# Reversing falling output tiles in device memory, and turning the last output pair around

## Chip, cores and metric

The kernel runs on one core of a Trainium2 chip. The metric is device time in microseconds (us) of one execution; shorter is better. The median of several executions is compared.

## The reference

Two blocks follow each other, for a batch of 4, 768 tokens, 8 heads of 64 (512 columns), all in float32. The first is attention in which a token sees its own and the neighbouring blocks of 32 tokens, the first and last block, and three sampled blocks. The second mixes with a Fourier transform, normalizes, and adds a two-layer network:

```
scores = scale * q @ k.T ; scores[~mask] = -1e9
attn   = softmax(scores) ; x = concat_heads(attn @ v)          # (4, 768, 512)
mixed  = real(fft(fft(x, axis=1), axis=2))
u      = x + mixed
un     = (u - mean(u)) / sqrt(var(u) + 1e-6)                   # per token
out    = u + maximum(un @ w_ch1, 0) @ w_ch2                    # 512 -> 2048 -> 512
```

## The kernel before

Queries of one batch are kept in six tiles of 128 tokens. Their order of rows (`_ORDER`, L53) is chosen for the Fourier step: tiles 0 to 2 are half 0 (tile buffer xA), tiles 3 to 5 half 1 (xB). Tiles 0, 1 and 5 hold tokens in rising order. Tiles 2, 3 and 4 are "falling": partition 0 holds one token, partitions 1 to 126 hold tokens in two interleaved runs that go down, and partition 127 a last one.

Attention of a batch runs in 24 slots (four pairs of heads, six slots each). Beside it the second block of the batch before runs: its steps stand in the queues `apart` (Fourier, normalization, transposes) and `late` (the products of the two layers, `quad` and `channels`), and a planner (`slot`, `gap`, `until`) places them between the attention's products by estimated durations. So all batches but the last share TensorE with the next batch's attention or, for batch 2, run after all attention is done; the last batch runs alone, with `outputs` in place of `channels`. Each engine executes its instructions in the order in which they are written. SP's queue issues nearly all transfers, also in that order: loads of q, k, v, the transposed activations' way through device memory (`far<-un`, L1020, then `unT<-far`, L1032), attention outputs (`row<-oT`, `x<-row`) and the output stores (L1292). It uses eight semaphores in turn, so a transfer also waits for the one eight before it.

`channels(r, half, m)` adds the second layer's product to tile m of one half and, in the last round, calls `store(half, m)`. For the batches before the last, half 0 is stored in the order 2, 0, 1 and half 1 in the order 0, 1, 2. `store` issues one transfer for every part of the tile's row order: a rising tile takes two of 64 rows (tile 5 takes four: 1, 48, 15 and 64 rows), a falling one three: 1 row, 126 rows, 1 row. The 126 rows are written by one transfer whose pattern in device memory has the two runs outermost ([2 runs, 63 rows going down, 512 columns]).

The token tiles xA and xB have two buffers each. `place` (L672, its copy is L681) writes attention outputs of batch b into the buffer of batch b - 2, so `slot` first works off what is left of that batch's half (`until(lambda: (b - 2, 0) in finished)`), and the copy waits for its stores.

In the last batch `outputs(r, m, after)` (L1335) computes a pair of output tiles, m of xA and m of xB, with seven products instead of eight (sums of blocks are formed by VectorE). `OUT` (L1303) gives the order of the pairs: 0, 1, 2 there. The last pair (`ends`) stores each half of the columns as soon as it is done: first xA's left half, then xB's left half (on ScalarE's queue) and right half, last xA's right half. So the last transfer of the program is a falling one (tile 2). After it comes the branch L1805 that skips a general version of the kernel.

Of the kernel before, what the change touches and what calls it, by code (L numbers as in the profile page):

```python
# [11 lines left out]
FP32 = mybir.dt.float32  # L12
# [5 lines left out]
ALU = mybir.AluOpType  # L18
# [62 lines left out]
def _rows(view, tile):  # L81

    got = []
    for t, p0, runs, jump, n, s0, step in _ORDER:
        if t != tile:
            continue
        at = view[s0:s0 + 1, :]
        row, col = list(at.ap[0])[0], list(at.ap[1])
        if jump > 0 > step:
            got.append((p0, runs * n, bass.AP(tensor=at.tensor, offset=at.offset,  # L90
                                              ap=[[jump * row, runs], [step * row, n], col])))
            continue
# [8 lines left out]
def kernel(  # L101
# [14 lines left out]
    nc = tc.nc  # L116

    B, H, S, D = q.shape
    DM = H * D
    FF = w_ch1.shape[1]  # L120
    P = 128
# [9 lines left out]
    T = C // 2  # L131
# [170 lines left out]
    def bit(n):  # L302
# [5 lines left out]
                      in_=bass.AP(tensor=_words(sampled_blocks, NB * NR), offset=0,  # L308
                                  ap=[[0, NB], [1, 2 * NB * NR]]))
# [138 lines left out]
    for w, w_sb in ((w_ch1, w1_sb), (w_ch2, w2_sb)):  # L448
        rows, cols = w.shape
        words = _words(w, rows * cols)  # L450
        for row in range(rows // P):
            for col in range(0, cols, WN):
                src = bass.AP(tensor=words, offset=2 * (row * P * cols + col),
                              ap=[[2 * cols, P], [1, 2 * WN]])
# [527 lines left out]
    z_at = [0.0, 0.0]  # L982
    rstd_at = deque()
    finished = set()
    folded = set()

    def mixer(b, xA, xB):
# [4 lines left out]
        tt = nc.vector.tensor_tensor  # L992
# [51 lines left out]
        t, s = {}, {}  # L1044
# [243 lines left out]

        def store(half, m, cols=slice(0, DM), queue=nc.sync):
            x = (xA, xB)[half]  # L1290
            for p0, cnt, rows in _rows(out[b][:, cols], T * half + m):
                queue.dma_start(out=rows, in_=x[p0:p0 + cnt, m, cols])  # L1292
            if cols.stop == DM:
                stored[half] += 1
            if stored[half] == T:
                finished.add((b, half))

        stored = [0, 0]
        last = b == B - 1
        OUT = (0, 1, 2) if last else (2, 0, 1)  # L1303
        out_of = (OUT, OUT if last else (0, 1, 2))
        o_t, o_s = {}, {}
        DH = DM // 2

        def block(r, k, n):
            return w2_sb[:, 8 * r + 4 * k:8 * r + 4 * k + 4, n * DH:n * DH + DH]
# [25 lines left out]
        def outputs(r, m, after):  # L1335

            if m == OUT[0]:
                output_left(m, 1)
                output_left(m, 2)
            a11, a12, a21, a22 = (hs[g, i][:, :, m * P:(m + 1) * P]  # L1340
                                  for i in range(2) for g in range(2))
            a0, a1 = xA[:, m, 0:DH], xA[:, m, DH:DM]
            b0, b1 = xB[:, m, 0:DH], xB[:, m, DH:DM]
            rights = {j: [o_t[j, 0], o_t[j, 1]] for j in (1, 2, 3, 4)}

            def product(pool, tag, a, c):
                ps = pool.tile([P, 512], FP32, tag=tag, name="yy")[:, 0:DH]
                for k in range(4):
                    nc.tensor.matmul(ps, a[:, k, :],  # L1349
                                     c[k // 2][:, k % 2, :] if isinstance(c, list) else c[:, k, :],  # L1350
                                     start=(k == 0), stop=(k == 3))
                busy("PE", 1.75)
                return ps

            def plus(to, a, c=None):
                tt(out=to, in0=a, in1=to if c is None else c, op=ALU.add)
                busy("DVE", 0.43)

            def ahead(j):
                if after is not None:  # L1360
                    output_left(after, j)

            ends = r == 1 and after is None
            u = sum_p.tile([P, DH], FP32, tag="oT", name="u")
            p1 = product(ps_m, "m", a11, block(r, 0, 0))
            nc.scalar.copy(out=u, in_=p1)
            plus(a0, p1)
            plus(a0, product(ps_m, "m", a12, block(r, 1, 0)))
            if ends:
                store(0, m, slice(0, DH))  # L1370
            if m == OUT[0]:
                output_left(m, 3)
                output_left(m, 4)
            plus(u, product(ps_t, "t", a21, rights[2]), u)
            plus(a1, u)
            plus(b0, product(ps_s, "s", a22, rights[4]))
            plus(u, product(ps_s, "s", o_s[m, 3], rights[3]), u)
            both = xB[:, m, :].rearrange("p (n d) -> p n d", n=2)
            tt(out=both, in0=both,
               in1=u.rearrange("p (o d) -> p o d", o=1).broadcast_to([P, 2, DH]), op=ALU.add)  # L1380
            busy("DVE", 0.7)


            if ends:
                store(1, m, slice(0, DH), nc.scalar)
            p5 = product(ps_o, "o", o_s[m, 1], rights[1])
            plus(b1, p5)
            if r == 1:
                store(1, m, slice(DH if ends else 0, DM))
            plus(a1, p5)  # L1390
            ahead(1)
            ahead(2)
            ahead(3)
            p3 = product(ps_m, "m", o_s[m, 4], block(r, 1, 1))
            plus(a1, p3)
            if r == 1:
                store(0, m, slice(DH if ends else 0, DM))
            ahead(4)

        fl = [[("tm"[h == 1 and m != 0], lambda h=h, m=m: un_flip(h, m), 0.6, 0.55, 0.0)  # L1400
# [10 lines left out]
              for m, us in (((1, 2), RIGHT), ((0,), COMBINE))]  # L1411
        le = [("d", lambda i=i: left(0, i), 0.0, 0.0, COMBINE) for i in (1, 3, 4)]
        after = ([fl[0][1], sp[1][1]] + le +
                 [fl[0][2], sp[1][2], wh[1][1], fl[0][0], sp[1][0], wh[1][2],
                  fl[1][1], fl[1][2], wh[1][0]] + ri[0] + [fl[1][0]] + ri[1])
        if not last:
# [13 lines left out]
        for r in range(0 if last else NF // 4):  # L1430
# [21 lines left out]
    needed = set()  # L1452
    state = {"paired": False, "total": None, "w": 0, "got": 0, "owed": 0.0, "ready": 0.0,
             "back": 0.0, "place": None,
             "alone": False, "drain": lambda: None}

    def channel_step():
        masks["by_pe"] = False
# [62 lines left out]
    def until(met, alone=False):  # L1521

        state["alone"] = alone
        while not met():
            if late:
                channel_step()
                soon = state.pop("soon", None)
                gap(2.0, start=soon)
            else:
                do_apart()  # L1530
        state["alone"] = False
# [24 lines left out]
    def w_loads():  # L1556
        while state["got"] < min(len(wchunks), state["w"] + len(W_ROOMS)):
            w_load(state["got"])
            state["got"] += 1

    def w_steps(sl):
        while state["w"] < min(len(wchunks), W_PACE * sl):
            w_round(state["w"])
            state["w"] += 1

    def slot(sl):
        phase, r = divmod(sl, SB)
        n, s = divmod(sl, SP)
        units = range(SLOT * sl, SLOT * sl + SLOT)
# [55 lines left out]
        if s >= ((4 if late else 5) if reuse else 3) and (n, 0) in oT_at and once(n):  # L1625
            b, j = pairs[n]
            at = oT_at[n, 0]
# [12 lines left out]
        if sl < B * SB and n % NP == 1 and s == 1:  # L1640
            b = pairs[n - 1][0]
            at = oT_at[n - 1, 1]
            if b >= 2:
                until(lambda: (b - 2, 1) in finished)
                at = when["PE"] + LEAVES
# [46 lines left out]
        while short and (not more or soon) and (  # L1692
# [5 lines left out]
            short.remove(item)  # L1698
            item[2]()
        w_loads()  # L1700
        w_steps(sl)
        table_step(sl)

# [32 lines left out]
    begin(B - 1)  # L1736
    state["drain"] = lambda: None
    until(lambda: len(finished) == 2 * B, True)
    ordered.close()

    def general():
# [4 lines left out]
        for b in range(B):  # L1748
            xs = [xp.tile([P, T, DM], FP32, tag=tag, name="x") for tag in ("xA", "xB")]
            for h in range(H):  # L1750
                qt = ld.tile([P, C, 2, D], FP32, tag="q", name="qg")
                for t in range(C):
                    for p0, cnt, rows in _rows(q[b, h], t):
                        nc.sync.dma_start(out=qt[p0:p0 + cnt, t, 0, :], in_=rows)
                nc.sync.dma_start(out=qt[:, :, 1, :],
                                  in_=k[b, h].rearrange("(p c) d -> p c d", p=P))
                vt = ldv.tile([P, C, D], FP32, tag="v", name="vg")
                nc.sync.dma_start(out=vt, in_=v[b, h].rearrange("(p c) d -> p c d", p=P))
                for half in range(2):
# [4 lines left out]
                    sl = slice(half * HS, (half + 1) * HS)  # L1764
# [3 lines left out]
                op = ps_o.tile([P, C, D], FP32, tag="o", name="og")  # L1768
                rs = sm.tile([P, C, 1], FP32, tag="r", name="rs", bufs=2)
                for t in range(C):  # L1770
                    s = ps_s.tile([P, 2, 512], FP32, tag="s", name="sg")
# [29 lines left out]
                step[1]()  # L1801
            for fn, _ in rest:
                fn()

    with tc.If(over > 0):  # L1805
        general()
# [37 lines left out]
```

## Time and profile before

| what | value |
|---|---|
| median of 3 runs | 1046.56 us (1045.99 to 1046.66) |
| the profiled execution | 1045.29 us, its span 1043.6 us |
| granted TensorE clock, mean | 0.994 |
| TensorE matmuls busy | 1018.6 us (98%) |
| VectorE, ScalarE, GpSimd busy | 683.2, 359.3, 257.7 us |
| transfers | 58.06 MB in 163582 packets, mean 56 GB/s |
| output stores (L1292) | 71 issued by SP, 4 by ScalarE |
| output stores of batch 0, 1, 2, 3 begin at | 389.6, 633.1, 866.3, 1010.0 us |

The span is the time from the first to the last instruction. A line of the timeline has start, length, engine, line of the kernel, operation, output and inputs, and in brackets how long the engine stood idle before it and what released it. SPq is SP's queue.

### The profile page before, as it was taken

Reading aid. Unit: us, or ns where it says so; the run is one execution under the profiler, and the core shown is the slowest. Engines: PE = TensorE matmul, PEld = TensorE weight load, DVE = VectorE, ACT = ScalarE, POOL = GpSimd, SP = SyncE. Lnnn points to the kernel's source line nnn. Section 1 sums busy time; section 2 is a strip of 40 time slices with the busy share of each in tenths; the row PEclk is TensorE's granted clock in tenths of the full one; section 3 lists DMA queues with packets and bytes.
Section 4 is the critical chain, followed back from the end, with each engine's and each line's share of the span. In section 5 each row is a group of like instructions: output and inputs, shape, how many; then the busy total and the mean of one; then the engine's idle time right before and its main releaser. Section 6 shows DMA issues by size and latency. Waiting matters only on the chain.

```text
span 1043.6 us, 12498 instructions
## 1 busy us (share of the span) xinstructions
PE 1018.6 (98%) x4382; PEld 537.0 (51%) x4382; DVE 683.2 (65%) x1246; ACT 359.3 (34%) x727; POOL 257.7 (25%) x287
## 2 busy tenths in 40 slices
PE   8999999999999999999999998999999999999996
PEld 4444345435565454444535653444444764578575
DVE  6899895978745646655677367665458475674663
ACT  6998765563021012433341111253220221210210
POOL 1000173662000203545560003256540221000000
PEclk9999999999999999999999999899999999999998
DMA  7767422291000143322320005521010001000001
GB/s 213 225 190 234 99 47 46 51 153 25 1 1 20 41 58 65 73 47 45 63 46 1 1 20 101 91 48 43 17 23 8 0 1 42 20 0 1 1 19 45
DMA packets 163582, 58.06 MB, mean 56 GB/s; under 512 B 144298, under 2 KB 154296, under 8 KB 163512
## 3 DMA queue, kind: packets, MB, share of 16 engines
q1 hardware_dynamic: 162216, 56.46, 24.1%
q10 hardware_dynamic: 1264, 0.72, 0.3%
q8 instruction: 36, 0.59, 0.2%
q14 instruction: 34, 0.28, 0.1%
q0 software_dynamic: 32, 0.01, 0.0%
HBM read 43.80 MB, written 13.37 MB: 55 GB/s over the span
## 4 chain that ended last, share of the span: by engine, by line
PE 84%; DVE 8%; DMA 2%; ACT 2%; SPq 2%; issue 1%; ACTq 0%; DVEq 0%
PE y L1281 20%; PE z L1116 16%; PE s L583 11%; PE o L657 9%; PE yp L1116 8%; PE yy L1349 7%; PE xp L1116 4%; PE zp L865 2%; PE sp L728 1%; PE s L593 1%; DMA far<-un 1%; ACT e L603 1%; DVE t L1070 1%; PE yz L1224 1%; DVE acc L638 1%
## 5 line engine op out<-in xcount | busy, mean ns | idle before, releaser
L643 POOL TENSOR_TENSOR acc<-acc,e 128x384 f32<-128x384 f32 x160 | 163.4, 1054 | 126.3 <-DVE e L613 106.7
L583 PE MATMUL s<-qT,kT 64*128 64x384 f32 x768 | 154.5, 518 | 9.5 <-DVE e L613 5.4
L657 PE MATMUL o<-e,vr 128*64 128x384 f32 x768 | 141.7, 497 | 0.0
L1281 PE MATMUL y<-w_sb,hB 128*128 128x512 f32 x264 | 118.9, 601 | 0.0
L1281 PE MATMUL y<-w_sb,hA 128*128 128x512 f32 x264 | 117.1, 595 | 0.0
L613 DVE TENSOR_TENSOR e<-s,mask 128x768 f32<-128x768 f32 x86 | 78.3, 950 | 53.9 <-ACT s L611 45.9
L583 PEld LDWEIGHTS s<-qT,kT 64*128 64x128 f32 x768 | 64.4, 187 | 90.0 <-ACT e L603 22.7
L1284 DVE TENSOR_TENSOR x<-y,x 128x512 f32<-128x512 f32 x66 | 45.6, 691 | 98.3 <-PE y L1281 98.1
L611 ACT ACTIVATE s<-s 128x768 f32<-128x768 f32 x86 | 65.1, 791 | 107.3 <-PE s L583 107.2
L603 ACT ACTIVATE e<-s 128x768 f32<-128x768 f32 x106 | 81.0, 814 | 54.2 <-PE s L593 32.9
L643 POOL TENSOR_TENSOR acc<-e 128x384 f32<-128x384 f32 x42 | 48.7, 1180 | 201.5 <-ACT e L603 121.9
L1116 PE MATMUL z<-unT,t 128*128 128x384 f32 x256 | 93.1, 486 | 0.0
L657 PEld LDWEIGHTS o<-e,vr 128*64 128x64 f32 x768 | 47.9, 136 | 69.4 <-issue 67.0
L1281 PEld LDWEIGHTS y<-w_sb,hB 128*128 128x128 f32 x264 | 49.6, 192 | 62.0 <-issue 61.3
L1121 DVE TENSOR_TENSOR hA<-z,hA 128x384 f32<-128x384 f32 x64 | 35.7, 557 | 69.8 <-PE z L1116 69.7
L1281 PEld LDWEIGHTS y<-w_sb,hA 128*128 128x128 f32 x264 | 49.2, 190 | 59.5 <-issue 55.7
L1125 ACT ACTIVATE hA<-hA 128x384 f32<-128x384 f32 x64 | 33.5, 523 | 121.8 <-DVE hA L1121 121.8
L1116 PEld LDWEIGHTS z<-unT,t 128*128 128x128 f32 x256 | 48.6, 190 | 34.1 <-DVE hA L1121 0.4
L1125 ACT ACTIVATE hB<-hB 128x384 f32<-128x384 f32 x64 | 33.5, 523 | 86.0 <-DVE hB L1121 86.0
L1136 ACT COPY hA<-xp 128x384 f32<-128x384 f32 x32 | 15.3, 477 | 129.3 <-PE xp L1116 129.3
L1116 PE MATMUL z<-t,w_sb 128*128 128x384 f32 x128 | 46.7, 487 | 1.5 <-DVE t L1070 1.5
L1116 PE MATMUL xp<-unT,w_sb 128*128 128x384 f32 x128 | 47.2, 492 | 0.0
(236 smaller groups left out, 1440.4 us busy)
## 6 DMA issues: line engine op xcount, KB each, us to landing
wraw<-in_moe_w_ch_dram SPq DMA_DIRECT2D x32, 512.0 KB
vr<-in_v_dram SPq DMA_DIRECT2D x30, 192.0 KB
far<-un SPq DMA_DIRECT2D x18, 256.0 KB
unT<-far SPq DMA_DIRECT2D x24, 192.0 KB
qb<-in_q_dram SPq DMA_DIRECT2D x44, 96.0 KB
kb<-in_k_dram SPq DMA_DIRECT2D x44, 96.0 KB
out_dram<-x SPq DMA_DIRECT2D x11, 252.0 KB
out_dram<-x SPq DMA_DIRECT2D x19, 128.0 KB
```

The lines of the kernel that those rows point to most:

```text
L583: nc.tensor.matmul(s[:, i, 0:HS], kT[rows, c * P:(c + 1) * P], qT[rows, queries], start=True, stop=u not in by_pe)
L603: nc.scalar.activation(out=e, in_=s[:, :, 0:HS], func=ACT.Exp, scale=scale)
L611: nc.scalar.activation(out=s[:, :, 0:HS], in_=s[:, :, 0:HS], func=ACT.Exp, scale=scale)
L613: nc.vector.tensor_tensor(out=e, in0=s[:, :, 0:HS], in1=m.broadcast_to([P, 2, HS]), op=ALU.mult)
L643: nc.gpsimd.tensor_add(out=acc[:, i, :], in0=start[:, i, :], in1=e[:, i, :])
L657: nc.tensor.matmul(o[D * i:D * i + D, :], vt[:, i, c, :], e[:, i, :], start=(c == 0), stop=(c == C - 1))
L1116: nc.tensor.matmul(to, a[:, k, :], c[:, k, :], start=(k == 0), stop=(k == ND // 2 - 1))
L1121: tt(out=to, in0=ps, in1=a, op=ALU.add)
L1125: nc.scalar.activation(out=h, in_=h, func=ACT.Relu)
L1281: nc.tensor.matmul(y, hs[0, half][:, l, m * P:(m + 1) * P], w2_sb[:, 4 * r + l, :], start=(l == 0), stop=(l == 3))
L1284: nc.vector.tensor_tensor(out=x[:, m, :], in0=y, in1=x[:, m, :], op=ALU.add)
L1349: nc.tensor.matmul(ps, a[:, k, :], c[k // 2][:, k % 2, :] if isinstance(c, list) else c[:, k, :], start=(k == 0), stop=(k == 3))
```

## The change

- `store` of a falling tile (2, 3, 4) of batches 0 to 2 no longer writes the output. `turn_round` writes its 128 rows to a scratch tensor in device memory, where the rows stand in the reverse order of the output: the pattern is [2 runs, 64 rows, 512 columns]. The rows of partition 0, which belong to the far end of the run, are written by single-row transfers: to the scratch tensor (tiles 2 and 5), or straight to the output (tile 3).
- When a half's tile 2 (`m == T - 1`) is stored, a copy `fall` is owed. It copies 128 rows (half 0) or 256 rows (half 1) from scratch to the output, device memory to device memory, with a row step of -1 in the output; its patterns have two halves of the columns outermost ([2 halves, n rows, 256 columns]). It goes out on SP's queue ahead of the next `store`, or at the end of a later slot.
- Single-row parts of a store are issued after the larger ones.
- The last batch takes its pairs in the order 2, 0, 1, so that the last pair is tiles 1 (rising, xA) and 4 (falling, xB). In that pair the products come in another order: xB's halves are finished and stored first (both on ScalarE's queue), then xA's right half, then its left half. Falling tiles of the last batch are stored as before.

```
+    owed = deque()
 ...
         def store(half, m, cols=slice(0, DM), queue=nc.sync):
             x = (xA, xB)[half]
-            for p0, cnt, rows in _rows(out[b][:, cols], T * half + m):
+            while owed:
+                owed.popleft()[1]()
+            falls = T * half + m in (T - 1, T, T + 1) and not last
+            if falls:
+                turn_round(half, m)
+            for p0, cnt, rows in sorted(_rows(out[b][:, cols], T * half + m), key=lambda i: -i[1]):
+                if falls and (cnt > 1 or p0 or m):
+                    continue
+                if not last and half == 1 and m == T - 1 and cnt == 1:
+                    rows = falling[1][2 * P:2 * P + 1, :]
                 queue.dma_start(out=rows, in_=x[p0:p0 + cnt, m, cols])
+            if not last and m == T - 1:
+                owed.append((state["slot"], lambda: fall(half)))
 ...
+        def turn_round(half, m):
+            if half not in falling:
+                falling[half] = far_p.tile([(1 + half) * P + 1, DM], FP32, tag=f"fall{half}",
+                                           name="falls", bufs=2)
+            rows = falling[half]
+            x = (xA, xB)[half][:, m, :]
+            at = rows[m * half * P:m * half * P + 1, :]
+            nc.sync.dma_start(out=bass.AP(tensor=at.tensor, offset=at.offset,
+                                          ap=[[DM, 2], [2 * DM, P // 2], [1, DM]]), in_=x)
+            if half == 0:
+                nc.sync.dma_start(out=rows[P:P + 1, :], in_=x[0:1, :])
+
+        def fall(half):
+            n = (1 + half) * P
+            src, to = falling[half][1:2, :], out[b][S // 2 * (1 + half) - 1:S // 2 * (1 + half), :]
+            nc.sync.dma_start(
+                out=bass.AP(tensor=to.tensor, offset=to.offset,
+                            ap=[[DM // 2, 2], [-DM, n], [1, DM // 2]]),
+                in_=bass.AP(tensor=src.tensor, offset=src.offset,
+                            ap=[[DM // 2, 2], [DM, n], [1, DM // 2]]))
 ...
-        OUT = (0, 1, 2) if last else (2, 0, 1)
+        OUT = (2, 0, 1)
 ...
+            if r == 1 and after is None:
+                plus(u, product(ps_t, "t", a21, rights[2]), u)
+                plus(a1, u)
+                plus(u, product(ps_s, "s", o_s[m, 3], rights[3]), u)
+                tt(out=both, in0=both,
+                   in1=u.rearrange("p (o d) -> p o d", o=1).broadcast_to([P, 2, DH]), op=ALU.add)
+                busy("DVE", 0.7)
+                plus(b0, product(ps_s, "s", a22, rights[4]))
+                store(1, m, slice(0, DH), nc.scalar)
+                p5 = product(ps_o, "o", o_s[m, 1], rights[1])
+                plus(b1, p5)
+                store(1, m, slice(DH, DM), nc.scalar)
+                plus(a1, p5)
+                plus(a1, product(ps_m, "m", o_s[m, 4], block(r, 1, 1)))
+                store(0, m, slice(DH, DM))
+                plus(a0, product(ps_m, "m", a12, block(r, 1, 0)))
+                store(0, m, slice(0, DH))
+                return
 ...
     def slot(sl):
+        state["slot"] = sl
 ...
         w_loads()
+        while owed and owed[0][0] < sl:
+            owed.popleft()[1]()
         w_steps(sl)
```

More of the change, by code (lines that the diff above doesn't have):

```diff
@@ L1290, in store @@
             x = (xA, xB)[half]
-            for p0, cnt, rows in _rows(out[b][:, cols], T * half + m):
+            while owed:
[8 more added lines that the diff above has]
+                    rows = falling[1][2 * P:2 * P + 1, :]
                 queue.dma_start(out=rows, in_=x[p0:p0 + cnt, m, cols])
-            if cols.stop == DM:
-                stored[half] += 1
-            if stored[half] == T:
+            if not last and m == T - 1:
+                owed.append((state["slot"], lambda: fall(half)))
+            stored[half] += cols.stop - cols.start
+            if stored[half] == T * DM:
                 finished.add((b, half))
+        falling = {}
+        def turn_round(half, m):
[17 more added lines that the diff above has]
+                            ap=[[DM // 2, 2], [DM, n], [1, DM // 2]]))
         stored = [0, 0]
         last = b == B - 1
-        OUT = (0, 1, 2) if last else (2, 0, 1)
+        OUT = (2, 0, 1)
         out_of = (OUT, OUT if last else (0, 1, 2))
@@ L1361, in ahead @@
                     output_left(after, j)
-            ends = r == 1 and after is None
             u = sum_p.tile([P, DH], FP32, tag="oT", name="u")
+            both = xB[:, m, :].rearrange("p (n d) -> p n d", n=2)
             p1 = product(ps_m, "m", a11, block(r, 0, 0))
@@ L1367, in outputs @@
             plus(a0, p1)
+            if r == 1 and after is None:
[16 more added lines that the diff above has]
+                return
             plus(a0, product(ps_m, "m", a12, block(r, 1, 0)))
-            if ends:
-                store(0, m, slice(0, DH))
             if m == OUT[0]:
@@ L1377, in outputs @@
             plus(u, product(ps_s, "s", o_s[m, 3], rights[3]), u)
-            both = xB[:, m, :].rearrange("p (n d) -> p n d", n=2)
             tt(out=both, in0=both,
@@ L1381, in outputs @@
             busy("DVE", 0.7)
-            if ends:
-                store(1, m, slice(0, DH), nc.scalar)
             p5 = product(ps_o, "o", o_s[m, 1], rights[1])
@@ L1388, in outputs @@
             if r == 1:
-                store(1, m, slice(DH if ends else 0, DM))
+                store(1, m)
             plus(a1, p5)
@@ L1396, in outputs @@
             if r == 1:
-                store(0, m, slice(DH if ends else 0, DM))
+                store(0, m)
             ahead(4)
@@ L1454 @@
              "back": 0.0, "place": None,
-             "alone": False, "drain": lambda: None}
+             "slot": 0, "alone": False, "drain": lambda: None}
     def channel_step():
@@ L1738 @@
     until(lambda: len(finished) == 2 * B, True)
+    assert not owed
     ordered.close()
@@ L1803, in general @@
                 fn()
+            while owed:
+                owed.popleft()[1]()
     with tc.If(over > 0):
```

## The prediction

> **What bounds the kernel now.** I read the page first (busy shares), then the waits, then the timeline around each group of output stores, and last the trace's records of DMA packets and of the semaphore increments with which a transfer lands.
>
> ```profile
> PE 1018.6 (98%) x4382; PEld 537.0 (51%) x4382; DVE 683.2 (65%) x1246; ACT 359.3 (34%) x727; POOL 257.7 (25%) x287
> ```
>
> TensorE is busy 98% of the span and works in a fixed order, so only what makes it idle, or what follows its last product, can move the time. Gaps between matmul records sum to 16.9 us; the longest by far is 4.52 us at 648.80. The view of the copy `place` (L681, PSUM to the token tile x) names what it waits for:
>
> ```profile
>   DMA far<-un: 8.7, 1
>   PE xt L680: 2.6, 4
>   DMA out_dram<-x: 1.9, 1
> ```
>
> The timeline around the long one (start us, length us, engine, line, operation; in brackets the idle time before it), SP's queue and then ACT and TensorE:
>
> ```profile
> 635.09 0.35 SPq L1020 DMA_DIRECT2D far<-un  x1
> 636.49 1.19 SPq L1292 DMA_DIRECT2D out_dram<-x  x2
> 637.79 0.53 SPq L1020 DMA_DIRECT2D far<-un  x1
> 641.98 3.96 SPq L1032 DMA_DIRECT2D unT<-far  x4
> 645.98 1.94 SPq L1292 DMA_DIRECT2D out_dram<-x  x2
> ```
>
> ```profile
> 650.26 0.48 ACT L681 COPY x<-xt 128x384 f32<-128x384 f32 x1 [8.70 <-DMA far<-un]
> 650.64 0.85 ACT L540 ACTIVATE kb<-kb 128x768 f32<-128x768 f32 x1
> ...
> 653.32 2.93 PE L583 MATMUL s<-qT,kT 64*128 64x384 f32 x8 [4.52 <-DVE e L613]
> ```
>
> The copy writes the xA buffer of batch 1, so it needs that batch's half-0 stores done. The last two (645.98 and 647.32) landed at 649.69 and 650.01; the copy follows 0.25 later. The name far<-un is wrong here: that transfer landed at 650.63. Behind the copy, in ACT's order, stand a square and the next exponential, then DVE's masking, then TensorE's scores: copy to scores is 3.06 us. So in this stage (call it batch 1) the end is set by SP's queue. Batch 0 has the same place with a little slack:
>
> ```profile
> 400.00 0.48 ACT L681 COPY x<-xt 128x384 f32<-128x384 f32 x1 [1.90 <-DMA out_dram<-x]
> ...
> 402.55 2.80 PE L657 MATMUL o<-e,vr 128*64 128x384 f32 x16
> ...
> 405.27 1.56 PE L583 MATMUL s<-qT,kT 64*128 64x384 f32 x8
> ```
>
> The stores landed at 399.40 and 399.71. TensorE is not idle; with 3.1 us from copy to scores the copy could start at 402.15 before the scores at 405.27 move. Slack: 2.15 us.
>
> **How stores of falling rows run.** A 126-row falling store shows two late semaphore increments, a 64-row one sixteen, a 15-row one fifteen: the count of DMA engines follows the outermost count in device memory (2, 64, 15), for 126 rows as such would allow 14. Alone, issue to landing is 7.9 us (633.38 to 641.29) against 2.3 to 2.9 for 64 rows. Packets on those two engines: 2 KB each 79 ns, 1 KB each 44 ns when queued up, plus 1.9 us of stalls for a store that starts fresh (1011.50 to 1018.41 is 6.9, 63 x 0.079 is 5.0). The other transfers use all 16 engines, so each has a share waiting behind these two: far<-un of 635.09 landed after 6.83 us, others of its kind after 2.6.
>
> **The change, part by part.**
>
> *Falling tiles to scratch (`turn_round`).* 128 rows again with an outermost count of 2: 64 packets of 2 KB per engine instead of 63, landing after 8.0 us. Per batch SP issues 15 instead of 17; its queue has gaps around these stores, so that is worth nothing.
>
> *The copy back (`fall`).* New: device memory to device memory, outermost count 2 on both sides, 1 KB packets, 128 per engine for half 0 and 256 for half 1. The Trainium skill, page "DMA: Bandwidth & Descriptors", section "Why a DMA increments its semaphore by 16 and not by 1", gives the engine count as the largest number up to 16 that divides the slowest dimension of both access patterns. By that rule these copies sit on two engines as well, which no row here shows for this kind of transfer; it speaks against the change. Price per packet: not below 44 ns (1 KB, SBUF to device memory); not above 88 (reading and writing one after the other). The v loads read 1.5 KB in 61 ns spacings, reading and writing together, so I take 44. The same page, section "Latency and other measured facts", has device-to-device copies at 207 to 214 GB/s each way over 16 engines; from this I estimate 79 ns, and by it the sum below would be about +35 us.
>
> *Its place in SP's queue.* half 0's `fall` is owed after tile 2's store, which comes first (order 2, 0, 1), and `store` issues what is owed before its own transfers. So it stands ahead of tile 0's and tile 1's stores, waits for `turn_round` to land, and its data stand ahead of theirs on engines 0 and 1. Exactly those stores release the copy L681.
>
> Batch 0. `turn_round` lands by 398.5 (before: 398.33, 398.51). `fall` issues at 398.6; first packet 1.3 later (1010.23 to 1011.50), 399.9. 128 x 0.044 + 1.9 of stalls: 407.5. Tile 0 and 1: 16 packets x 0.079: 408.8; landing 0.3: 409.1. Before 399.7, so 9.4 late; less slack 2.15: **7.2 us** of new TensorE idling. After the 4.52 us gap the granted clock is 0.50 from 652.3 to 659.1; the 5.8 us of work in it lose 2.9. A gap of 7 should do the same: **2.9**. Bounds: 5.0 (no stalls, no clock loss) to 15.7.
>
> ```profile
> 640.00:653.00 13.00, 8.80 (x41) 3.51 (x37) 8.10 (x11) 4.24 (x8) 4.42 (x4) 0.97 0.77 150
> 653.00:655.00 2.00, 1.68 (x6) 1.03 (x8) 1.13 (x2) 1.19 (x3) 0.00 (x0) 0.50 1.18 175
> ```
>
> (The column before the last two is the granted clock.)
>
> Batch 1. `turn_round` issued 633.06, landed 641.2; `fall` issues 641.3, packets 642.6 to 650.2. Behind it on the two engines: tile 0's store 0.64, far<-un 0.64, four unT<-far (96 packets of 128 B each per engine, 11.7 ns: 4.5), tile 1's store 0.64, landing 0.3: 656.9. Before 650.0: **6.9 us**, no slack; the clock loss is paid already. Bounds 4.7 to 12.5. What follows (unT<-far of half 1, kb loads) is shifted along with TensorE.
>
> Half 1's `fall` (256 packets, some 13 us) is issued at the end of the next slot. The qb load behind it (680.26) is wanted at 700.30, row<-oT ahead of a normalization after 783: hidden by that slack; if it were gone, up to 9 us. Batch 2 runs its stores with nothing waiting; no cost, except that no slot follows, so its half-1 `fall` is issued by the last batch's first store.
>
> *The end.* Before:
>
> ```profile
> 1034.22 3.32 SPq L1292 DMA_DIRECT2D out_dram<-x  x7
> ```
>
> ```profile
> 1033.57 1.89 PE L1349 MATMUL yy<-w_sb,os 128*128 128x256 f32 x8
> ...
> 1035.50 0.42 DVE L1356 TENSOR_TENSOR x<-yy,x 128x256 f32<-128x256 f32 x1 [0.97 <-PE yy L1349]
> ```
>
> The falling store issued at 1036.34 ends its packets at 1041.27; SP passes that wait at 1041.71, 1.3 us after it could (its branch at 1037.60 takes 2.55 until 1040.15); the span ends 1.9 later. With tile 1 last, two 64-row stores end it: SP branches at 1037.1 and nothing is left to wait for: 1.7 us gained, were engines 0 and 1 free. The seven products keep their durations; one 0.18 us wait for a PSUM bank goes, which the branch covers. But from 1011.2 the engines have: `fall` 256 x 0.044 + 1.9, tile 2 and tile 3 falling 5.0 each, tile 5 and tile 0 0.63 each, tile 4 in two halves on ACT's queue 5.6, the last two stores 0.4: 30.5 us, to 1041.7, where it was 1041.3. So **+0.4**; bounds -1.7 to +11.5.
>
> Sum: 7.2 + 2.9 + 6.9 + 0.4 = 17.4 us. The profiled execution took 1045.29 (span 1043.6 and 1.7 around it), 1.27 under the median of 1046.56; so about 1062.7 for such an execution and 1064.0 as median.
>
> **Rivals.**
> 1. *Everything on sixteen engines* (128 rows divide by 16, 126 don't). It decides if `turn_round` lands before 636.5, some 3 us after issue as 64-row stores do. Then far<-un lands at 637.7, unT<-far starts 3 us earlier, the gap at 648.80 shrinks by 3.0 and no longer halves the clock (2.9), and the end gives 1.7: 7.6 gained, 1039. Against it: the [63,2] stores that used two engines though 126 has divisor 14. Chance 0.08.
> 2. *Copy back on sixteen, `turn_round` on two.* Only SP's wait is left: batch 0 stores land at 403.5 (3.8 late, 1.65 after slack), batch 1 starts unT<-far at 643.7 instead of 641.98 (1.7), the end gives 1.7: +1.7, 1048.2. Nothing speaks for the difference between the two transfers but their kind. Chance 0.06.
> 3. *The copies L681 are not what binds* and the delays hide; only the end counts: 1045 to 1047. Against it: both copies start 0.25 to 0.29 after the stores land. Chance 0.05.
>
> The forecast keeps 0.81.
>
> **How the numbers follow.** About 0.2% (2 us) can be told from no change. Faster: rival 1 and a little of rival 3, 0.09. Same: rival 2 and the rest of 3, 0.10. Slower 0.81. The forecast's own bounds are 5.0 + 4.7 - 1.7 = 8.0 (1054.6) and 15.7 + 12.5 + 11.5 = 39.7 (1086). Reading and writing overlap in the v loads, so I stop at 1080 above; below, 1051 takes in some hiding not seen. Left out: the rivals and the top, 2 in 10.
>
> **What would show it.** Right: L681's DMA waits grow to about 11 and 15.6 us; a gap of some 7 us before the scores at 405 with granted clock 0.50 behind it; the gap at 649 near 11 us; `fall` landing some 9 and 15 us after issue, with two late increments; the last stores landing near 1042 plus the shift. Wrong: `fall` with sixteen increments, or tile 1's stores landing within 2 us of where they did against the products around them.

## The result, and the profile after

The changed kernel takes 1071.34 us (median of 4 runs, 1071.17 to 1071.61) against 1046.34 of the kernel before on the same chip: ratio 1.0239, 95% interval 1.0222 to 1.0257. The forecast was 1064.0 with a range of 1051 to 1080, so direction and range hold, and the middle is 7 us too low.

The page, its line of busy times:

```profile
span 1069.5 us, 12491 instructions
...
PE 1021.1 (95%) x4382; PEld 538.3 (50%) x4382; DVE 683.4 (64%) x1246; ACT 359.6 (34%) x727; POOL 258.0 (24%) x287
```

TensorE does the same 4382 products, in the same order up to the pairs of the last batch, in 2.5 us more busy time; the span is 25.9 us longer. So most of the loss is idle time, and the start of the i-th matmul in one trace can be subtracted from its start in the other. By the times of the trace of before, that difference stays within 0.1 us of 0 up to the product at 405.27, is 5.81 there and 8.74 from 408.6 on, stays there until 653.32, jumps to 14.98, and is 14.5 from 659 to the last product. Behind the last product, 8.1 us to the end of the span became 19.5. Three places, then, to the hundredth: 8.74 + 5.72 + 11.42 = 25.88.

The copy into the token tile (L681) names the first two:

```profile
  DMA far<-un: 14.9, 1
  DMA out_dram<-x: 9.8, 1
  PE xt L680: 2.6, 4
```

Before, these were 8.7 and 1.9. The timeline of batch 0 (start, length, engine, line, operation, output and input; in brackets the idle time before it), SP's queue, then ACT and TensorE:

```profile
389.84 0.74 SPq L1322 DMA_DIRECT2D falls<-x  x1
390.62 0.91 SPq L1325 DMA_DIRECT2D falls<-x  x1
398.30 0.66 SPq L1331 DMA_DIRECT2D out_dram<-falls  x1
399.06 3.76 SPq L1302 DMA_DIRECT2D out_dram<-x  x4
```

```profile
407.97 0.48 ACT L681 COPY x<-xt 128x384 f32<-128x384 f32 x1 [9.79 <-DMA out_dram<-x]
...
411.08 1.65 PE L583 MATMUL s<-qT,kT 64*128 64x384 f32 x4 [5.67 <-DVE e L613]
```

SP issues nothing from 391.5 to 398.30: it waits for `turn_round` (issued 389.84, landed 398.28). `fall` lands at 406.35, and the stores of tiles 0 and 1, issued behind it, at 406.68 to 407.66 instead of 399.71 at the latest. The copy starts 0.31 after the last of them, the scores 3.11 after the copy. Then the half clock (the column before the last two):

```profile
411.00:413.00 2.00, 1.92 (x6) 1.14 (x8) 0.89 (x2) 1.11 (x4) 0.00 (x0) 0.50 0.67 130
413.00:415.00 2.00, 2.00 (x6) 0.54 (x3) 1.00 (x2) 1.37 (x2) 0.00 (x0) 0.50 0.40 63
```

Batch 1, which begins 8.7 later than in the trace of before:

```profile
641.80 0.56 SPq L1322 DMA_DIRECT2D falls<-x  x1
...
649.86 0.66 SPq L1331 DMA_DIRECT2D out_dram<-falls  x1
650.62 2.11 SPq L1302 DMA_DIRECT2D out_dram<-x  x2
652.83 0.53 SPq L1021 DMA_DIRECT2D far<-un  x1
653.47 7.36 SPq L1033 DMA_DIRECT2D unT<-far  x4
660.93 1.82 SPq L1302 DMA_DIRECT2D out_dram<-x  x2
```

```profile
665.24 0.48 ACT L681 COPY x<-xt 128x384 f32<-128x384 f32 x1 [14.93 <-DMA far<-un]
...
668.30 1.01 PE L583 MATMUL s<-qT,kT 64*128 64x384 f32 x2 [10.76 <-DVE e L613]
```

The last two stores of tile 1 land at 664.79 and 665.02 (before: 649.69 and 650.01, so 6.3 late when the 8.74 of batch 0 are taken off), and the copy follows 0.22 behind. The name far<-un in the bracket is again not the releaser: that transfer landed at 665.62, after the copy had begun.

The end, SP's queue and ACT's over the last batch, and then SP's alone as it stands in a window that begins at 1035:

```profile
1024.46 40.34 SPq L1302 DMA_DIRECT2D out_dram<-x  x16
1045.23 3.52 ACTq L1302 DMA_DIRECT2D out_dram<-x  x6
```

```profile
1050.44 14.36 SPq L1302 DMA_DIRECT2D out_dram<-x  x13
```

Sixteen stores from 1024.46, of which thirteen begin at 1050.44 or later: SP issued three and then stood still for 24 us. SP's waits between 1024 and 1066 (total, times, longest) put that down to an earlier store that had to land, not to the data:

```profile
SPq L1302 <- DMA out_dram<-x: 30.5, 4, 24.3
```

At 1050.44 the last product was over (1049.92), and four of the last batch's six tiles had still to be issued; the last transfer landed at 1066.38.

### The profile page after: what moved, and what is told of

It is laid out like the page before. It is cut to its first block, busy times and chain, and to the rows that moved or that the text cites. A ratio compares the mean times of both kernels' runs of the same rounds, so it can differ in the third digit from the quotient of the medians.

```text
span 1069.5 us, 12491 instructions
## 1 busy us (share of the span) xinstructions
PE 1021.1 (95%) x4382; PEld 538.3 (50%) x4382; DVE 683.4 (64%) x1246; ACT 359.6 (34%) x727; POOL 258.0 (24%) x287
## 4 chain that ended last, share of the span: by engine, by line
PE 83%; DVE 7%; ACT 3%; DMA 2%; SPq 2%; issue 1%; ACTq 0%; DVEq 0%
PE y L1282 20%; PE z L1117 15%; PE s L583 11%; PE o L657 9%; PE yp L1117 8%; PE yy L1385 6%; PE xp L1117 4%; PE zp L865 2%; PE sp L728 1%; PE s L593 1%; ACT e L603 1%; DMA far<-un 1%; DVE t L1071 1%; PE yz L1225 1%; DVE acc L638 1%
```

## Experiments

**The theories.** A: the 14.5 us in the middle come from where half 0's copy back stands (in SP's queue, and on its two DMA engines) ahead of the stores that release L681; the 11.4 us at the end have another cause, a semaphore. The trace's records give, for each transfer, the semaphore that it raises and those that it waits for. SP's fourth store of the last batch (the one row of tile 5) waits for semaphore 117 and starts at 1050.44. The transfer before it on 117 is not SP's: it is ScalarE's store of xB's left half, issued at 1045.23, landed at 1050.42. So the eight semaphores are not for SP's queue alone, as the description of the kernel has it: they serve the transfers of both queues in turn, in the order in which the built program lists them. For the last batch the records give the turn as 117 ScalarE (126 rows), 100 SP (64), 102 ScalarE (1), 111 SP (48), 112 ScalarE (1), 113 SP (15), 115 ScalarE (126), 116 ScalarE (1), 117 SP (1). ScalarE's stores of the last pair stand ahead of and between SP's stores of tile 5, which are ready 20 us earlier. Why the built program lists them so early is not shown. Rivals: the added traffic itself costs, wherever it stands (middle); falling rows back up on two engines, or the new last pair costs as such (end).

| run | last matmul ends | end of span behind it | median | ratio to before, 95% interval |
|---|---|---|---|---|
| before | 1035.5 | 8.1 | 1045.3 to 1046.5 | 1 |
| after | 1049.9 | 19.5 | 1071.34 | 1.0239, 1.0222 to 1.0257 |
| end_on_sp | 1049.9 | 6.5 | 1057.88 | 1.0118, 1.0103 to 1.0134 |
| fall_late | 1034.9 | 19.8 | 1057.30 | 1.0114, 1.0098 to 1.0129 |
| scratch_alone | 1050.6 | 12.9 | 1065.45 | 1.0184, 1.0168 to 1.0201 |
| last_pair_alone | 1034.9 | 8.3 | 1044.74 | 0.9991, 0.9982 to 1.0000 |
| round16 | 1042.3 | 8.1 | 1049.48 | 1.0031, 1.0019 to 1.0043 |
| fall16 | 1039.2 | 6.4 | 1047.91 | 1.0017, 1.0008 to 1.0027 |
| both16 | 1032.4 | 8.3 | 1042.35 | 0.9962, 0.9949 to 0.9975 |
| late_both16 | 1030.3 | 8.1 | 1040.12 | 0.9943, 0.9930 to 0.9957 |
| late_on_sp | 1035.6 | 6.3 | 1043.28 | 0.9976, 0.9967 to 0.9985 |
| last_pair_on_sp | 1034.9 | 7.5 | 1044.33 | 0.9992, 0.9983 to 1.0001 |
| late_both16_moved | 1030.1 | 6.4 | 1038.10 | 0.9927, 0.9914 to 0.9941 |

(us; the first two columns of numbers are from each kernel's profiled execution, the ratios are to the kernel before on the same chip. The ranges of "before" are its medians on the chips used here. The profiled executions lie within 0.9 us of their kernel's median, but round16's is its slowest, 1052.19, 2.7 above the median.)

### end_on_sp: the last pair's stores on one queue

```
-                store(1, m, slice(0, DH), nc.scalar)
+                store(1, m, slice(0, DH))
 ...
-                store(1, m, slice(DH, DM), nc.scalar)
+                store(1, m, slice(DH, DM))
```

> As the changed kernel, but the last pair's two xB stores go out on SP's queue instead of ScalarE's. Theory A (the extra 11.5 us behind the last product come from SP standing still: its tile-5 transfer waits for the completion semaphore that was handed to a ScalarE store which is issued only at 1045): with all stores on one queue no transfer waits for a later one, the time from the last matmul to the end of the span falls from 19.6 us to 6 to 9 us, and the median to 1058 to 1061. Rival B (the end is a backlog of falling rows on two DMA engines): the same rows fall, so the 19.6 us stay within 2 us and the median within 1069 to 1072. By both the TensorE gaps at 405 (5.7 us) and 657 (10.8 us) stay.

Measured: the last matmul ends where it did, both gaps stand (5.79 and 11.03 us), and the end shrinks from 19.5 to 6.5 us. The median is 0.1 under the range given. SP's stores of the whole last batch, and its waits for earlier stores between 1024 and 1052:

```profile
1024.48 27.05 SPq L1302 DMA_DIRECT2D out_dram<-x  x22
```

```profile
SPq L1302 <- DMA out_dram<-x: 0.5, 1, 0.5
```

Twenty-two stores in 27 us instead of sixteen in 40; the longest stretch without an issue, 7.9 us up to 1036.62, is a wait for a tile that DVE finishes. The rows, their patterns and their two engines are those of the changed kernel; rival B falls.

### fall_late: the copy back behind the stores

```
-            while owed:
+            while owed and half == 1:
                 owed.popleft()[1]()
```

> As the changed kernel, but half 0's copy back is no longer issued ahead of the stores of tiles 0 and 1: it goes out at the end of the next slot. Theory A (what delays both middle stages is the place of the copy back in SP's queue and on its two engines ahead of the stores that release L681): tile 0's and 1's stores land where they did before, the gap at 405 goes, the one at 649 is again about 4.5 us, the last matmul ends within 2 us of 1035.5, and the median is 1056 to 1059, the end keeping its 19 to 20 us (ScalarE's stores still hold semaphores that SP waits for). Rival B (the cost is the added traffic itself: 2.4 MB more, and two engines busy for 8 us more): the copy runs 10 us later into the next loads, at least half of the 14.5 us stays, median 1064 or more.

Measured: the gap at 405 is gone, the one at 649 is 4.11 us, the last matmul ends at 1034.9; all 14.5 us are back, with the same traffic. SP's queue in batch 0:

```profile
396.54 1.11 SPq L1302 DMA_DIRECT2D out_dram<-x  x2
398.59 0.69 SPq L1331 DMA_DIRECT2D out_dram<-falls  x1
```

The stores at 396.54 land at 399.40 and 399.71, to the hundredth as before the change, and `fall` goes out behind them; it still takes 8.45 us. Rival B falls here too. The end keeps its 19.8 us:

```profile
1009.41 40.63 SPq L1302 DMA_DIRECT2D out_dram<-x  x16
1030.17 3.56 ACTq L1302 DMA_DIRECT2D out_dram<-x  x6
```

This run shows the semaphore's mechanism a second time, at another transfer. The built program's order differs a little, so SP now stands one transfer earlier, before the 15-row store of tile 5; and the same holds in scratch_alone, where ScalarE stores parts of tile 5 as before the change and SP stands before tile 1's first store. From the records of the three traces:

```
kernel         SP's store that stood    semaphore  ScalarE's store before it on that semaphore
after          1 row,   start 1050.44   117        126 rows, issued 1045.23, landed 1050.42
fall_late      15 rows, start 1035.36   117        126 rows, issued 1030.17, landed 1035.34
scratch_alone  64 rows, start 1050.45   112        64 rows,  issued 1048.34, landed 1050.38
```

### scratch_alone and last_pair_alone: each half of the change by itself

scratch_alone has `turn_round` and `fall`, with `OUT`, `ends` and the last pair as in the kernel before:

```
-        OUT = (2, 0, 1)
+        OUT = (0, 1, 2) if last else (2, 0, 1)
```

> The reversal through device memory alone; the last batch's order of pairs and its last pair as before the change. Theory A: both middle gaps as in the changed kernel (last matmul 14 to 15 us later than before), and behind it SP still waits once for a semaphore that a ScalarE store holds (here before tile 1's stores), so that the last falling halves start some 3 us later against the last product: median 1062 to 1066. Rival B (what costs at the end is the new last pair): the end is that of before, 8.1 us behind the last matmul, median 1060 to 1061.

last_pair_alone stores the tiles of batches 0 to 2 as before, and has the new last pair:

```
-            if cols.stop == DM:
-                stored[half] += 1
-            if stored[half] == T:
+            stored[half] += cols.stop - cols.start
+            if stored[half] == T * DM:
 ...
-        OUT = (0, 1, 2) if last else (2, 0, 1)
+        OUT = (2, 0, 1)
```

> The new order of pairs and the new last pair alone; output tiles of batches 0 to 2 stored as before the change. Theory A (the last pair itself gains, since the last transfers are 64-row ones; its loss came with the way in which the copy back changed the semaphores): all matmuls but the last pair's where they were, the end 6 to 8 us behind the last matmul instead of 8.1, median 1044 to 1046.5. Rival B (the new last pair costs, whatever the stores before it): 19 us behind the last matmul, median 1057 to 1058.

Measured: the reversal alone has both gaps (5.89 and 10.89 us) and, without the new last pair, still 12.9 us at the end instead of 8.1. Rival B of that run (the end as before) falls. The new last pair alone costs nothing: median 1.0 us lower, an interval that just touches no change. In the turn of the semaphores, ScalarE's stores (102 to 116) here come behind all of SP's stores of the other tiles, and no transfer waits for a later one. The products end 0.6 us earlier in the profiled execution, but 0.56 of this is there before the last pair begins, so the pair's products save 0.04. Its end is 8.3 us, not the 6 to 8 expected: the falling half stored last from ScalarE's queue (issued 1032.46) lands after 8.50 us, and SP's 64-row stores, issued around it, after 5.2 to 5.9.

### round16, fall16 and both16: which two-engine transfer costs what

All three start from end_on_sp. round16 writes `turn_round` as two transfers whose outermost count is 64:

```
+            for r in range(2):
-            nc.sync.dma_start(out=bass.AP(tensor=at.tensor, offset=at.offset,
-                                          ap=[[DM, 2], [2 * DM, P // 2], [1, DM]]), in_=x)
+                nc.sync.dma_start(out=bass.AP(tensor=at.tensor, offset=at.offset + r * DM,
+                                              ap=[[2 * DM, P // 2], [1, DM]]),
+                                  in_=x[r * P // 2:(r + 1) * P // 2, :])
```

> As end_on_sp (last pair's stores on SP's queue), and turn_round writes its 128 rows as two transfers of 64 rows, which use sixteen DMA engines; the copy back stays on two. Theory A (the sum: SP waits 8 us for turn_round to land, then the copy back holds two engines for 8 us ahead of the stores that release L681): turn_round lands 3 to 3.5 us after its issue, the copy back then takes its 8 us from 393.5 to 401.5 in batch 0, so tile 0's and 1's stores land by 402.5, about the end of the slack: gap at 405 at most 1 us. In batch 1 the stores land within 4 us of before. Median 1043 to 1049. Rival C (it is the copy back alone that costs, wherever it starts): the gaps shrink by no more than 2 us each and the median stays at 1053 or more.

fall16 cuts the columns of `fall` into 16 parts instead of 2, on both sides:

```
-                            ap=[[DM // 2, 2], [-DM, n], [1, DM // 2]]),
+                            ap=[[DM // 16, 16], [-DM, n], [1, DM // 16]]),
```

> As end_on_sp, and the copy back is cut into sixteen column parts (128 bytes a packet), so that sixteen engines do it; turn_round stays on two. Theory A: only SP's wait for turn_round is left; tile 0's and 1's stores of batch 0 land 4 to 6 us later than before, less 2.15 us of slack: 2 to 4 us; batch 1 1.7 to 4 us: median 1047 to 1053. Rival D (the copy back costs by its bytes and packets, 2048 of them for half 0 instead of 256, not by the number of its engines): it lands 8 us or more after its issue, as in end_on_sp, and the median stays within 3 us of 1058 or goes above it.

both16 has both edits.

> As end_on_sp with both: turn_round as two transfers of 64 rows and the copy back in sixteen column parts; its place in SP's queue stays ahead of the stores. Theory A: turn_round lands after 3 to 3.5 us, the copy back 3 to 5 us after that, no TensorE gap at 405; in batch 1 far<-un and unT<-far no longer stand behind falling rows on two engines, so the gap of 4.5 us at 649 shrinks and may vanish: median 1037 to 1043, under the kernel before. Rival D (copies in device memory cost by their packets): 1046 or more.

Measured: in fall16 the copy back lands 3.6 us after its issue, with sixteen increments, for 2048 packets of 128 bytes, and the gap at 405 is 1.74 us; rival D falls. The Trainium skill, page "DMA: Bandwidth & Descriptors", section "Why a DMA increments its semaphore by 16 and not by 1", has the engine count follow the slowest dimension; these runs agree, for copies in device memory too (outermost 2: two late increments, outermost 16: sixteen). In round16 the copy back takes 8.14 us as before, and here the expectation missed: the gap at 405 is 3.20 us and not at most 1, because `turn_round` lands 5.5 us after its issue, not 3 to 3.5. Fifteen of its increments come within 3.9 us (the transposed activations' loads of 388 are still in front of it), the last one 1.6 us later; a packet of 16 KB that loads instructions takes 1.45 us from 392.63 on, but the records don't name its engine, so that it held up this one is an inference. The copy back then starts at 395.62 and the stores land at 405.06. Its median lies 0.5 over the range given; rival C, with 1053 or more, falls all the same. In both16 the two transfers' terms vanish, and the gap of the kernel before shrinks as well:

```profile
651.25 2.35 PE L583 MATMUL s<-qT,kT 64*128 64x384 f32 x8 [2.58 <-DVE e L613]
```

By the end of the last matmul in the profiled executions, from both16 (1032.4): the copy back on two engines costs 9.9 us (round16, its slowest execution), `turn_round` on two 6.8 (fall16), both on two (end_on_sp) 17.5. Medians less the end behind the last matmul give 7.4, 7.5 and 17.4. Each of the two costs some 7 us or more; how nearly they add is open.

### late_on_sp and late_both16: the place

late_on_sp has the edits of fall_late and of end_on_sp; late_both16 has these and both of sixteen engines.

> The two single corrections together: half 0's copy back at the end of the next slot (as fall_late), and the last pair's stores on SP's queue (as end_on_sp); falling rows and the copy back still on two DMA engines. Theory A (two separate causes): the last matmul ends at 1034.9 as in fall_late, the span 6.5 us behind it as in end_on_sp: span 1041.4, median 1042.5 to 1044.5. Rival E (the two share something, two engines that are full at the end): the sum isn't reached, median 1046 or more.

> As both16, with half 0's copy back issued at the end of the next slot instead of ahead of the stores of tiles 0 and 1. Theory A: all three causes are gone; no gap at 405, in batch 1 only what the loads and the exponentials behind them need, the end 6.5 us behind the last product: median 1036 to 1042. Rival D: the 2048 small packets hold all sixteen engines while the next loads want them, and the median is 1044 or more.

Measured: late_on_sp has the end of the last matmul of fall_late (within 0.8 us) and the end of end_on_sp, and comes out 0.24% under the kernel before: the two causes are separate, and they are all of the loss. late_both16 leaves 1.35 us of the gap at 649, and the granted clock stays at 1.00 behind it:

```profile
649.52 1.78 PE L583 MATMUL s<-qT,kT 64*128 64x384 f32 x8 [1.35 <-DVE e L613]
```

```profile
  DMA far<-un: 5.5, 1
  PE xt L680: 2.5, 4
```

L681 waits 5.5 us where it waited 8.7. But its end is 8.1 us, not the 6.5 expected, though the last store lands 4.45 us behind the last matmul as in end_on_sp (4.52).

### last_pair_on_sp and late_both16_moved: the end's remainder

After the branch L1805, SP passes the eight transfer semaphores one after the other, 0.07 us apiece. In late_both16 there are 1.80 us between two of them, in both16 1.97 between another two, in round16 1.56 behind the eighth; the semaphores waited for had risen before (in late_both16 the one row on 116 landed at 1031.04, SP passes it at 1036.79). Counted in SP's part of the built program (the traces don't hold this count), each pause stands before the same instruction, number 1488 counted from 0. late_both16_moved shifts what is behind the branch, by instructions that the branch skips:

```
-                nc.sync.dma_start(out=vt, in_=v[b, h].rearrange("(p c) d -> p c d", p=P))
+                for i in range(16 if (b, h) == (0, 0) else 1):
+                    n = P // 16 if (b, h) == (0, 0) else P
+                    nc.sync.dma_start(out=vt[i * n:i * n + n],
+                                      in_=v[b, h].rearrange("(p c) d -> p c d", p=P)[i * n:i * n + n])
```

> As late_both16, with 12 more instructions in SP's program, in the general version that the branch skips (one load in it is cut into 16 parts); nothing that runs differs. Theory G (the 1.8 us pause between two of SP's last semaphore instructions falls at a fixed place of SP's program, its 1488th instruction, where the next block of code is brought in): the code behind the branch now begins at instruction 1494, the pause goes, the span ends 6.3 us behind the last matmul instead of 8.1, median 1037.8 to 1039. Rival H (the pause is a wait for a transfer that the records don't show): 8.1 us stay, median 1039.7 to 1040.7.

last_pair_on_sp is last_pair_alone with the edit of end_on_sp.

> As last_pair_alone (no scratch tensor), with the last pair's xB stores on SP's queue. Theory A (with stores of two queues the 1 KB rows share two engines with the 64-row stores and land 2 us later): the last store lands 4.5 us behind the last matmul instead of 6.5. By the place of a pause in SP's code alone (seen at the 1488th instruction of SP's program in both16, late_both16 and round16; here that is the 19th after the branch) about 1.8 us are given back in the last steps: median 1044 to 1045. If there is no such pause: 1042.5 to 1043.5. Rival F (the queue makes no difference): the last landing stays at 6.5 us, median 1044.7 or more.

Measured: the pause is gone, the end is 6.4 us instead of 8.1, and the median is 1038.10, 2.0 us under late_both16, though the added code never runs. Theory G predicted it; H falls. The DMA records, which mark transfers of instructions, bear G out. In the eight runs with all stores of the last pair on SP's queue, four such packets of 8 KB follow the branch within 3.4 us. The four runs with a pause (round16, both16, late_both16, last_pair_on_sp) have a fifth, 0.6 to 0.9 us behind the pause; the four without a pause don't. That SP waited for code stays an inference, since this packet comes behind the pause and not in it.

In last_pair_on_sp the last store lands 4.4 us behind the last matmul instead of 6.5, as expected, so the second queue costs 2 us here (rival F falls); how the two queues hold one another up is not shown. By the trace the pause stands before the 19th instruction behind the branch, the place that was named, and is 1.0 us long, not 1.8: its length varies.

late_both16_moved is the fastest of the kernels: ratio 0.9927 to the kernel before, interval 0.9914 to 0.9941, some 7.6 us. late_on_sp, both16 and late_both16 also come out under the kernel before.

## Why the prediction was right, and where it was off

- *Two engines for `turn_round` and `fall`.* Right. `turn_round` lands after 8.44 us in batch 0 and 7.80 in batch 1 (8.0 forecast); `fall` [128,2] shows two late increments, 0.09 and 0.01 us apart in batches 0 and 1. Its price was a little high: it lands after 8.05 and 8.13 us (9 forecast), the 256-row one after 12.85 to 13.46 (15). The difference of the two, 4.7 to 5.4 us for 128 packets, gives 37 to 42 ns a packet where the sum took 44. The estimate from the figure of the Trainium skill, page "DMA: Bandwidth & Descriptors", section "Latency and other measured facts", was 79. The runs decide for the smaller price, at two engines.
- *Batch 0.* Forecast 7.2 + 2.9 = 10.1, measured 5.8 + 2.9 = 8.7 (the shift at the gap, and what the half clock adds behind it, from 5.81 to 8.74). The place, the releasing stores, the slack and the clock of 0.50 are as forecast; the 1.4 us are `fall` and the stores behind it, which landed at 407.66 and not 409.1.
- *Batch 1.* Forecast 6.9, measured 5.7: the stores land 6.3 us late, the gap grows from 4.52 to 10.76, and some 0.5 us come back behind it. L681's waits of 9.8 and 14.9 us against the 11 and 15.6 named tell the same. Half 1's copies cost nothing, as forecast: the difference holds at 8.74 and at 14.5 behind them.
- *Which of the two binds.* The sum took both in a chain, SP's wait for `turn_round` and then the copy. The runs give each by itself (6.8 to 7.5 us and 7.4 to 9.9, last matmul), and the chain 17.5. Taking the copy out of the chain by its place alone (fall_late) gives back all that the change cost in the middle.
- *The end.* This term failed: +0.4 forecast, +11.4 measured. It went wrong twice. The backlog on engines 0 and 1 that it summed up begins with half 1's `fall` of batch 2, "issued by the last batch's first store": in the queue it does stand right before that store, but nothing in front of it waits for the last batch, so SP issues it at 909.93, as soon as the rows that it copies have landed (909.88), and it is through at 923.06. With all stores on SP's queue the end is shorter than before (6.5 against 8.1), so the forecast backlog was not there. And what did hold up the end, a semaphore of SP's queue handed to a ScalarE transfer that is issued later, is in no line of the working: it takes the eight semaphores for SP's alone. The sign named for the end, last stores near 1042 plus the shift (1056.5), did not show: the last one landed at 1066.38. That the measured 11.4 equals the upper bound given there (11.5) is chance: that bound was a price for the backlog.
- *The last pair.* Forecast 1.7 us of gain "were engines 0 and 1 free". With SP's queue alone it is there: the end shrinks from 8.1 to 6.3 to 6.5 us (late_on_sp, end_on_sp). With ScalarE's stores it is not (8.3).
- *The sum.* 17.0 for the middle against 14.5, 0.4 for the end against 11.4. The two misses have opposite signs, which is why 25.9 us of span came out only 8.5 over the 17.4. With the end as in end_on_sp the time is 1057.88, inside the range as well, so the range held without speaking for the term of the end. The lower bounds 5.0 and 4.7 don't follow from their terms: 7.2 and 6.9 less 1.9 of stalls are 5.3 and 5.0, which makes the lower sum 8.6 and not 8.0.
- *The rivals.* Rival 1 put the case with sixteen engines everywhere at 7.6 us of gain. both16 is that case, made by hand: 4.0 by its ratio, since the gap at 649 shrank by 1.9 and not 3.0, the half clock behind it got shorter (3.4 us instead of 6.8; 0.56 to 0.58 from 652 to 656) but did not go, and the pause took the end's gain. Rival 2 gave +1.7 for the copy on sixteen alone; fall16 shows 1.8 by its ratio. Rival 3 is excluded by fall_late.

## What to carry to other kernels

Before a transfer is put into a queue, look at who stands behind it there: the same copy, with its wait for `turn_round`, cost 14.5 us ahead of the stores that released a buffer, and nothing one slot later. Count in how many DMA engines a pattern's outermost dimension can be cut before pricing it, and cut it by hand where it is 2; with all stores on one queue, that turned a loss into a gain here (both16). Where two queues share completion semaphores, check that no early transfer of one is numbered behind a late one of the other, and put both on one queue if it is.

## What the runs showed of the hardware that was not expected

- A queue that waits for a semaphore raised by another queue's later transfer stops everything behind it: 24 us without an issue in the changed kernel, 25 in fall_late, 12 in scratch_alone, each time before a different transfer.
- A pause of 1.0 to 2.0 us in SP's code at an all but fixed place of its program; moved away by instructions that are skipped, it shortened the end by 1.7 us.
- In the gap of 10.76 us the granted clock fell to 0.50 already inside it and stayed there for some 10 us, from about 662.9 to 673.1 by the two lines at its edges, while in batch 0 (a gap of 5.67) it lasted 6.8 us. So the longer gap's half clock covered only some 5 us of products, and its price did not grow with it:

```profile
662.00:664.00 2.00, 0.00 (x0) 0.00 (x0) 0.00 (x0) 0.00 (x0) 0.00 (x0) 0.72 1.26 188
664.00:666.00 2.00, 0.00 (x0) 0.00 (x0) 0.00 (x0) 0.76 (x2) 0.00 (x0) 0.50 0.78 290
...
672.00:674.00 2.00, 2.00 (x5) 0.83 (x4) 1.83 (x2) 0.07 (x1) 0.00 (x0) 0.72 1.25 129
```

- Over all runs the half clock before the last product came in lengths of 3.4, 6.8 and 10.2 us: none behind gaps of 1.35 to 1.74 us, 3.4 behind 2.58 to 4.11 and 4.60, 6.8 behind 4.52 and 5.2 to 7.7, 10.2 behind 10.8 to 11.0. Three runs (fall_late, late_on_sp, late_both16) have one of 3.4 us more between 883 and 892, which costs 1.2 us, where the others, with the same short gaps of 1.16 and 0.73 us, have none; what decides this is not shown.
